# First units of an attention stage in another order, with products that keep TensorE busy between them, before two mixture layers

## The chip, the cores and the metric

One Trainium2 chip, one core of it. The metric is the device time of one execution in microseconds (us); less is better. TensorE (PE) multiplies, with its weight loads (PEld) beside it; VectorE (DVE), ScalarE (ACT) and GpSimd (POOL) work on tiles, and SyncE (SP) issues the DMAs. Each engine takes its instructions in order.

## The reference

A gated linear attention with a running maximum (2 batches, 8 heads, 768 steps, head size 40) feeds two gated layers (1536 tokens, 320 wide, 1536 hidden), all in float32:

```python
for t in range(S):
    m_new = np.maximum(f_gate[:, :, t] + m, i_gate[:, :, t])
    f_stab = np.exp(f_gate[:, :, t] + m - m_new)
    i_stab = np.exp(i_gate[:, :, t] - m_new)
    C = f_stab * C + i_stab * (v k^T)
    n = f_stab * n + i_stab * k
    y[:, :, t] = sigmoid(o_gate) * (C q) / max(|n q|, 1)
x = rms_norm(y) * rms_g
x = (silu(x @ w_gate) * (x @ w_val)) @ w_out
x = (sigmoid(x @ w_gate2) * (x @ w_val2)) @ w_out2
```

The three lines for C, n and y are shortened here; f_stab and i_stab stand for each batch and head.

## The kernel before

**Attention.** The 768 steps are cut into 6 chunks of 128. A unit is one chunk of one batch, all 8 heads; there are 12, and unit u is chunk u // 2 of batch u % 2. Units 0 and 1 need no state from earlier chunks. The running maximum is a scan on DVE: `g_first` scans the first 128 steps (from the small load `fi0`), `g_max` (L178) the other 640. For chunks 1 to 5 the maximum has to lie with one row for each batch, head and chunk (80 rows of 129). Before, `g_move` (L182) writes it to a DRAM tensor `mD` and `g_back` (L186) reads it as 80 rows into `mR`; `g_rest` (L159 to L168) then makes the decay rows of all later chunks. `g_part` splits them into three bf16 parts (two on ACT, L196, one on DVE, L200), and `g_send` (L205) moves the parts to the tiles `rows3` with six DMAs from SP.

A unit goes through: `a_bcast0`/`a_bcast0b` (units 0, 1) or `a_bcast_pe` (later ones; L277, L280), products that lay decay rows over the 128 partitions; `a_exp` (ACT; L313 or L307); `a_scores` (L323, from the tile `qk`); `a_weigh` (DVE, L330); `a_out` (L343, from the tile `nat`, and L339 with the state); `a_wv`, `a_state` (L368), `a_update` (L379) for the state; `a_norm1` to `a_norm3` and `a_flip` (L423 to L425), `a_xt` (ACT, L430; DVE, L431), which put the normed rows transposed and split into `xT`. The causal mask of units below `LATE` is two mask products (L261) ahead of the others; from `LATE` on POOL zeroes the upper triangle after the exponential (L309, two of 128x512).

**Layers.** Tokens are taken in groups of two units; a step is one group with one block of 128 hidden units (12 blocks): `up1` (L460, 16 products of 256 columns), `act1` (ACT L489, DVE L490 and L491, ACT L492, POOL L493) and `dn1` (L471 to L473). The first group (visit 0) goes over the 12 blocks while their weights arrive. A block is two pieces of 544 KB, 24 pieces a layer. A piece is loaded to a raw buffer `wraw` (`w_load`, L98, three buffers); ACT decodes it (`w_pre`: L102 and L109), DVE joins the bits (`w_bits`, L113, last reader of the raw buffer), ACT casts (`w_hi`, L122), DVE subtracts (`w_lo`, L126). Later visits find the weights resident.

**What sets the order.** Everything up to the two `a_xt` of units 0 and 1 is written out by hand in `tc.manual_schedule`, each call adding its instructions at the end of its engines' queues (below: the opening). `keep_warm(n)` there puts n products of 512 columns on PE whose result nobody reads (L673). What follows is placed by a scheduler from due times (`want`). SP's queue is in order too: a DMA that waits holds up all behind it. A DMA takes one of eight semaphores in turn, so it also waits for the DMA eight places earlier.

Of the kernel before, what the change touches and what calls it, by code (L numbers as in the profile page):

```python
# [45 lines left out]

LATE = 4

# [10 lines left out]
def attention_then_two_moe(tc, fi, fir, qk, qt3, nat, w1, w2, rms_g, consts, out):  # L59
# [93 lines left out]
    parts = room[0][0:RR, again + 3 * L:again + 15 * L // 2].bitcast(BF16).rearrange("p (k n) -> p k n", k=3)  # L153
    ph = early[0:BH, 768:768 + L]
    col0, colR = early[:, 896:896 + 2 * BH], small(128, RR, "colR")
# [24 lines left out]

    def g_move():
        nc.sync.dma_start(out=mD, in_=mS[:, L:])  # L182

    def g_back():
        win = bass.AP(tensor=mD.tensor, offset=mD.offset, ap=[[S - L + 1, BH], [L, NR], [1, L + 1]])
        nc.sync.dma_start(out=mR, in_=win)  # L186

    def g_rest():
        g_cum(fiR[:, 0, :], fiR[:, 1, :], mR, phR, uR, RR, False)
        g_aw(fiR[:, 1, :], mR, phR, uR, aR, wsR, RR)  # L190

# [50 lines left out]
    def a_load(u, parts=(0, 1, 2, 3)):  # L242
        d = X.setdefault(u, {})
        if 0 in parts:
            d["qk"] = ap.tile([QR, 2, 4, L], F32, tag="qk", name="qk")
            nc.sync.dma_start(out=d["qk"], in_=qk[u])
        if 1 in parts:
            d["nat"] = ap.tile([128, NAT], F32, tag="nat", name="nat")
            nc.sync.dma_start(out=d["nat"][:, 9 * D:], in_=nat[u, :, 9 * D:])
        if 3 in parts:  # L250
            nc.sync.dma_start(out=d["nat"][:, 0:9 * D], in_=nat[u, :, 0:9 * D])
        if u >= B and 2 in parts:
            d["qt"] = ap.tile([KR, NG, L], F32, tag="qt", name="qt")
            nc.sync.dma_start(out=d["qt"], in_=qt3[u])
# [181 lines left out]
    def a_flip(u):  # L436
        X[u]["T"] = flip(X[u]["y"], X[u]["y"][:, 256:DP])
# [99 lines left out]
    def act2(g, m, gt, vl):  # L537
        if G2[g][1] == 2:
            th = mp.tile([128, 256], F32, tag="th", name="th")
            hT = hts[1, g, m] = mp.tile([128, 2, 256], F32R, tag="hT", name="hT", bufs=3)  # L540
        else:
            th = p2[0].tile([128, 512], F32, tag="th2", name="th2")
            hT = hts[1, g, m] = p2[0].tile([128, 2, 512], F32R, tag="hT2", name="hT2", bufs=3)
# [93 lines left out]
    with tc.manual_schedule(engines=set(engines)):  # L637
        nc.vector.memset(junk, 0.0)
        nc.sync.dma_start(out=fi0, in_=fi[:, :, 0:L])
        nc.scalar.dma_start(out=fiS, in_=fi[:, :, L:])  # L640
        a_load(0, (0,))
        w_load(0, 0, 0)
        nc.scalar.copy(tiny, junk[:, 0:1])
        for t, fill in ((ident, 1.0), (identb, 1.0)):
# [33 lines left out]
        g_max()
        w_pre(0, 0, 0)
        w_load(0, 0, 1)  # L680
        a_load(1, (0,))
        a_load(0, (1,))
        g_move()
        nc.sync.dma_start(out=fiR, in_=fir)
        g_back()
        w_load(0, 1, 0)
        a_load(1, (1,))
        w_load(0, 1, 1)
        nc.sync.dma_start(out=gB, in_=rms_g.partition_broadcast(128))
        nc.sync.dma_start(out=cst, in_=consts)  # L690
        a_load(0, (3,))
# [4 lines left out]
        w_bits(0, 0, 0)
        a_load(1, (3,))
        a_scores(0)
        keep_warm(wm[1])
        a_weigh(0)  # L700
        a_gate(0)
        w_hi(0, 0, 0)
        w_pre(0, 0, 1)
# [8 lines left out]
        a_scores(1)
        g_rest()
        a_out(0)
        a_wv(0)
        w_pre(0, 1, 0)
        g_exp()
        g_part(0)
        g_part(1)
        for k in range(3):  # L720
            g_send(k)
        a_weigh(1)
        w_hi(0, 0, 1)
        w_lo(0, 0, 1)
        a_gate(1)
        g_dec()
        a_norm1(0)
        a_norm1b(0)
        keep_warm(wm[3])
        a_out(1)  # L730
        a_norm1(1)
        a_norm1c(0)
        a_norm1b(1)
        a_norm2(0)
        a_bcast_pe(2)
        a_norm1c(1)
        a_norm2(1)
        keep_warm(wm[4])
        g_cols()
        a_norm3(0)  # L740
        a_flip(0)
# [123 lines left out]
```

## Time and profile before

| | us |
|---|---|
| three runs | 528.14, 524.8, 527.47; median 527.47 |
| profiled execution, its own time | 524.49 |
| span in that profile, first to last instruction | 522.7 |
| outside the span | 1.8 |

The profile is one execution. Its views used here: busy time in chosen stretches, the instructions of an engine in order of time (start, length, count, idle time before it and what ended it), groups of instructions by line, and the chain that ended last. A clock of 1.00 is 2.4 GHz on TensorE, 0.50 is 1.2 GHz. SPq is SP issuing a DMA; the length there is the issuing, not the transfer.

### The profile page before, as it was taken

Reading aid. Unit: us, or ns where it says so; the run is one execution under the profiler, and the core shown is the slowest. Engines: PE = TensorE matmul, PEld = TensorE weight load, DVE = VectorE, ACT = ScalarE, POOL = GpSimd, SP = SyncE. Lnnn points to the kernel's source line nnn. Section 1 sums busy time; section 2 is a strip of 40 time slices with the busy share of each in tenths; the row PEclk is TensorE's granted clock in tenths of the full one; section 3 lists DMA queues with packets and bytes.
Section 4 is the critical chain, followed back from the end, with each engine's and each line's share of the span. In section 5 each row is a group of like instructions: output and inputs, shape, how many; then the busy total and the mean of one; then the engine's idle time right before and its main releaser. Section 6 shows DMA issues by size and latency. Waiting matters only on the chain.

```text
span 522.7 us, 9043 instructions
## 1 busy us (share of the span) xinstructions
PE 503.7 (96%) x3576; PEld 466.8 (89%) x3576; DVE 260.4 (50%) x540; ACT 232.0 (44%) x518; POOL 105.3 (20%) x164
## 2 busy tenths in 40 slices
PE   7889899999999999999999899999999999999996
PEld 5668799999999999999999899998888888888996
DVE  5668789744255445557665646533233233222332
ACT  4667889733233333326576657442222222221322
POOL 7013135443243243232221211110000000000000
PEclk9769979999999999999999999999999999999999
DMA  6588787711041030102153242000000010000100
GB/s 193 182 255 298 246 262 231 240 55 41 1 112 44 25 114 16 41 2 85 35 198 113 92 165 87 1 1 25 1 1 2 0 51 0 1 0 1 51 1 26
DMA packets 15752, 43.09 MB, mean 82 GB/s; under 512 B 1822, under 2 KB 6734, under 8 KB 15710
## 3 DMA queue, kind: packets, MB, share of 16 engines
q1 hardware_dynamic: 15518, 42.27, 25.4%
q8 instruction: 28, 0.46, 0.4%
q10 hardware_dynamic: 192, 0.25, 0.1%
q14 instruction: 14, 0.11, 0.1%
HBM read 40.32 MB, written 2.01 MB: 81 GB/s over the span
## 4 chain that ended last, share of the span: by engine, by line
PE 76%; DMA 10%; ACT 6%; DVE 5%; issue 2%; SPq 0%; ACTq 0%; DVEq 0%
PE up L460 34%; DMA wraw<-in_w_dram 9%; PE sc L460 9%; PE dn L471 5%; PE dn L473 5%; PE dn L472 5%; PE at L343 4%; PE sc L323 2%; DVE wT L113 2%; PE at L471 2%; PE at L472 2%; PE at L473 2%; ACT wT L102 2%; ACT wH L122 2%; ACT wraw L109 1%
## 5 line engine op out<-in xcount | busy, mean ns | idle before, releaser
L460 PE MATMUL up<-xT,wH 128*128 128x256 f32 x940 | 165.4, 290 | 4.2 <-DVE th L491 4.0
L460 PEld LDWEIGHTS up<-xT,wH 128*128 128x128 f32 x940 | 136.0, 192 | 7.5 <-DVE th L491 5.4
L460 PE MATMUL up<-xT,wL 128*128 128x256 f32 x564 | 101.2, 287 | 0.3 <-DVE wL L126 0.3
L493 POOL TENSOR_TENSOR hT<-th,hT 128x256 fp32r<-128x256 f32 x72 | 57.7, 802 | 152.0 <-ACT hT L492 112.7
L460 PEld LDWEIGHTS up<-xT,wL 128*128 128x128 f32 x564 | 82.3, 192 | 0.7 <-DVE wL L126 0.5
L471 PE MATMUL dn<-wH,hT 128*128 128x320 f32 x184 | 58.1, 316 | 0.0
L490 DVE SCALAR_TENSOR_TENSOR th<-th,up 128x256 f32<-128x256 f32 x72 | 30.1, 418 | 56.2 <-ACT th L489 55.8
L472 PE MATMUL dn<-wL,hT 128*128 128x320 f32 x184 | 57.4, 313 | 0.0
L473 PE MATMUL dn<-wH,hT 128*128 128x320 f32 x184 | 56.9, 316 | 0.0
L544 ACT ACTIVATE th<-up 128x256 f32<-128x256 f32 (+1 forms) x48 | 23.4, 488 | 72.8 <-PE up L460 72.8
L545 DVE SCALAR_TENSOR_TENSOR th<-th,sc 128x512 f32<-128x512 f32 x24 | 16.5, 687 | 64.1 <-PE sc L460 63.9
L546 ACT CAST hT<-th 128x256 fp32r<-128x256 f32 (+1 forms) x48 | 24.6, 513 | 49.9 <-DVE th L545 49.8
L489 ACT ACTIVATE th<-up 128x256 f32<-128x256 f32 x72 | 27.3, 380 | 41.3 <-PE up L460 39.9
L109 ACT ACTIVATE wraw<-wraw 128x544 int32<-128x544 uint16 x48 | 34.0, 708 | 25.4 <-DMA wraw<-in_w_dram 25.0
L492 ACT CAST hT<-th 128x256 fp32r<-128x256 f32 x72 | 29.1, 404 | 34.6 <-DVE th L491 34.6
L113 DVE SCALAR_TENSOR_TENSOR wT<-wT,wraw 128x544 int32<-128x544 int32 x48 | 36.9, 772 | 12.8 <-ACT wT L102 7.7
L547 DVE TENSOR_TENSOR hT<-th,hT 128x256 fp32r<-128x256 f32 (+1 forms) x48 | 28.1, 585 | 25.0 <-ACT hT L546 24.9
L126 DVE TENSOR_TENSOR wL<-wT,wH 128x544 fp32r<-128x544 f32 x46 | 34.2, 770 | 7.1 <-ACT wH L122 6.9
L471 PEld LDWEIGHTS dn<-wH,hT 128*128 128x128 f32 x184 | 35.0, 190 | 1.2
L102 ACT ACTIVATE wT<-wraw 128x544 f32<-128x544 f32 x48 | 33.2, 702 | 6.2 <-DMA wraw<-in_w_dram 5.9
L472 PEld LDWEIGHTS dn<-wL,hT 128*128 128x128 f32 x184 | 34.9, 190 | 0.9
L473 PEld LDWEIGHTS dn<-wH,hT 128*128 128x128 f32 x184 | 34.3, 189 | 0.3 <-issue 0.2
(184 smaller groups left out, 821.5 us busy)
## 6 DMA issues: line engine op xcount, KB each, us to landing
wraw<-in_w_dram SPq DMA_DIRECT2D x48, 544.0 KB, 4.8
qk<-in_qk_dram SPq DMA_DIRECT2D x12, 416.0 KB
nat<-in_nat_dram SPq DMA_DIRECT2D x12, 324.0 KB, 2.8
nat<-in_nat_dram SPq DMA_DIRECT2D x12, 180.0 KB, 6.3
qt<-in_qt_dram SPq DMA_DIRECT2D x10, 180.0 KB, 2.8
out_dram<-x2n SPq DMA_DIRECT2D x11, 160.0 KB, 1.9
rows<-x2n SPq DMA_DIRECT2D x6, 30.0 KB
gB<-in_rms_g_dram SPq DMA_DIRECT2D x1, 160.0 KB
```

The costliest lines, as they stand in the source:

```text
L102: nc.scalar.activation(t.bitcast(F32), wraw[moe, m, p][:, :, 1].bitcast(F32), AF.Prelu, scale=2.0 ** -112, alpha=2.0 ** 32)
L109: nc.scalar.activation(raw[:, :, 0], top, AF.Copy, scale=2.0 ** -13, bias=2.0 ** -14 - 0.5)
L113: nc.vector.scalar_tensor_tensor(out=t, in0=t, scalar=3, in1=raw[:, :, 0], op0=ALU.logical_shift_left, op1=ALU.bitwise_or)
L126: nc.vector.tensor_tensor(out=wL[moe, m][:, sl], in0=wT.pop((moe, m, p)).bitcast(F32), in1=wH[moe, m][:, sl].bitcast(F32), op=ALU.subtract)
L460: mm = nc.tensor.matmul(o, lhsT=a, rhs=b, start=(n == 0), stop=(n == 7))
L471: nc.tensor.matmul(o, lhsT=hi, rhs=wo[0], start=first, stop=False)
L472: nc.tensor.matmul(o, lhsT=hi, rhs=wo[1], start=False, stop=False)
L473: pe_last[0] = nc.tensor.matmul(o, lhsT=lo, rhs=wo[0], start=False, stop=last)
L490: nc.vector.scalar_tensor_tensor(out=th, in0=th, scalar=1.0, in1=gt, op0=ALU.add, op1=ALU.mult)
L492: nc.scalar.copy(hT[:, 0, :], th)
L493: nc.gpsimd.tensor_tensor(out=hT[:, 1, :], in0=th, in1=hT[:, 0, :].bitcast(F32), op=ALU.subtract)
L547: nc.vector.tensor_tensor(out=hT[:, 1, :], in0=th, in1=hT[:, 0, :].bitcast(F32), op=ALU.subtract)
```

## The change

The opening is written anew: all loads of units 0 and 1 and the first four weight pieces are issued ahead of the computation; the maximum is scanned later; its 80 rows are made by five products with selection matrices (`selR`) into PSUM instead of the way through DRAM; ACT does the exponentials and the decay rows ahead of most weight pieces; the keep-warm products stand at other places (6, 5, 4, 8, 4 of them; before 6, 2, 0, 5, 4 and none at the last two places). The states of units 0 and 1 are placed earlier (that of unit 0 in the opening, that of unit 1 first thing after it). `LATE` goes from 4 to 2, so units 2 and 3 are masked on POOL and lose two mask products each. Half of the `rows3` transfers go out from POOL. `wraw` has four buffers (and `th2`, of the second layer, one instead of two). `qk` is 104 partitions of which 64 to 103 and 0 to 39 carry data; now the two ranges of 40 are loaded (320 KB) by two DMAs, before all 104 (416 KB) by one.

```diff
-LATE = 4
+LATE = 2
-    uld=9.62, sl=9.1, fl=-6.46, wm=(6, 2, 0, 5, 4, 0, 0), st=1.2,
+    uld=9.62, sl=9.1, fl=-6.46, wm=(6, 5, 4, 8, 4), st=1.2,
...
-        t = wraw[moe, m, p] = mp.tile([128, WP, 2], I32, tag="wraw", name="wraw", bufs=3)
+        t = wraw[moe, m, p] = mp.tile([128, WP, 2], I32, tag="wraw", name="wraw", bufs=4)
...
-    def g_move():
-        nc.sync.dma_start(out=mD, in_=mS[:, L:])
-
-    def g_back():
-        win = bass.AP(tensor=mD.tensor, offset=mD.offset, ap=[[S - L + 1, BH], [L, NR], [1, L + 1]])
-        nc.sync.dma_start(out=mR, in_=win)
+    def g_win():
+        m = psum("dn")[0:RR, 0:L + 1]
+        for c in range(NR):
+            nc.tensor.matmul(m, lhsT=selR[:, c, :], rhs=mS[:, L * (c + 1):L * (c + 2) + 1], start=(c == 0), stop=(c == NR - 1))
+        mR.append(m)
...
-    def g_send(k):
+    def g_send():
         n = H * NR
-        for b in range(B):
-            nc.sync.dma_start(out=rows3[b][k * n:(k + 1) * n].rearrange("p q l -> p (q l)"), in_=parts[b * n:(b + 1) * n, k])
+        for k in range(3):
+            for b, q in ((0, nc.sync), (1, nc.gpsimd)):
+                q.dma_start(out=rows3[b][k * n:(k + 1) * n].rearrange("p q l -> p (q l)"), in_=parts[b * n:(b + 1) * n, k])
...
-            nc.sync.dma_start(out=d["qk"], in_=qk[u])
+            for r in (0, 64):
+                nc.sync.dma_start(out=d["qk"][r:r + D], in_=qk[u, r:r + D])
...
-        a_bcast0(u, "sc")
+        a_bcast0(u, "up" if u == B else "sc")
...
-            th = mp.tile([128, 512], F32, tag="th2", name="th2")
+            th = mp.tile([128, 512], F32, tag="th2", name="th2", bufs=1)
...
-            [a_scale, a_bcast_pe, a_exp] if u > B else [a_scale, a_exp],
+            [a_scale, a_bcast_pe, a_exp],
```

(In the `th2` lines the pool is the second layer's own, `p2[0]`.) The opening, by its calls from the first computation on; loads stand ahead of it:

```python
keep_warm(6); a_bcast0(0); keep_warm(5); g_first(); a_bcast0b(0, 0); g_first_a(); a_bcast0b(0, 1); a_exp(0)
g_max(); a_scores(0); g_win(); a_weigh(0); g_first_ws(); w_pre(0, 0, 0); a_bcast0(1); a_bcast0b(1, 0); a_bcast0b(1, 1)
a_gate(0); g_rest(); a_exp(1); a_wv(0); a_out(0); w_bits(0, 0, 0); g_exp(); a_scores(1); g_part(0); a_norm1(0)
a_weigh(1); a_state(0); w_pre(0, 0, 1); g_part(1); a_norm1b(0); a_norm1c(0); g_send(); a_out(1); a_norm2(0)
w_hi(0, 0, 0); a_gate(1); w_bits(0, 0, 1); a_norm3(0); keep_warm(4); a_flip(0); a_norm1(1); a_norm1b(1); a_norm1c(1)
a_xt(0); w_lo(0, 0, 0); w_hi(0, 0, 1); g_dec(); a_update(0); a_norm2(1); w_pre(0, 1, 0); keep_warm(8); g_cols()
a_norm3(1); keep_warm(4); a_flip(1); w_lo(0, 0, 1); a_xt(1); w_bits(0, 1, 0); w_hi(0, 1, 0); w_lo(0, 1, 0)
```

PE before, from unit 1's mask products to unit 0's `a_out` (L266 feeds unit 1's exponentials, L229 makes a column of weights, L323 are unit 1's scores, L343 is unit 0's `a_out`):

```order
L261 LDWEIGHTS masks
L261 MATMUL up<-masks 128x512
L261 LDWEIGHTS masks
L261 MATMUL up<-masks 128x512
L266 MATMUL up<-x2n,ident 128x128 x8
L229 MATMUL at<-ident,x2n 128x16
L323 MATMUL sc<-qk 128x128 x8
L343 MATMUL at<-nat,E 128x41 x8
```

PE with the change, from unit 0's scores on:

```order
L323 MATMUL sc<-qk 128x128 x8
L183 MATMUL dn<-x2n,early 80x129 x5
L228 MATMUL at<-ident,x2n 128x16
L261 LDWEIGHTS masks
L261 MATMUL up<-masks 128x512
L261 LDWEIGHTS masks
L261 MATMUL up<-masks 128x512
L266 MATMUL up<-x2n,ident 128x128 x8
L343 MATMUL at<-nat,E 128x41 x8
L323 MATMUL sc<-qk 128x128 x8
```

The five products L183 come right behind unit 0's scores, and unit 0's `a_out` (L343) now stands ahead of unit 1's scores.

PE before, around the first step of visit 0 (unit 1's state is L368 with nat, unit 2 is L297, L323 and L339):

```order
L425 MATMUL at<-ident,y 128x128
L368 MATMUL at<-wv,nat 120x123 x2
L368 MATMUL at<-wv,nat 120x82
L460 MATMUL up<-xT,wH_211 128x256 x4
L460 MATMUL up<-xT,wL_212 128x256 x3
L460 MATMUL up<-xT,wH_211 128x256 x5
L460 MATMUL up<-xT,wL_212 128x256 x3
L460 MATMUL up<-xT,wH_211 128x256
L460 MATMUL up<-xT,wH_365 128x256 x4
L460 MATMUL up<-xT,wL_366 128x256 x2
L368 MATMUL at<-wv,nat 120x123 x2
L368 MATMUL at<-wv,nat 120x82
```

PE with the change, the last rows ahead of the first step (all of unit 2 but the state's addition):

```order
L323 MATMUL sc<-qk 128x128 x8
L297 LDWEIGHTS wide
L297 MATMUL at<-rows_0_72,wide 120x128
L297 LDWEIGHTS wide
L297 MATMUL at<-rows_0_72,wide 120x128
L297 LDWEIGHTS wide
L297 MATMUL at<-rows_0_72,wide 120x128
L339 MATMUL at<-St_77,qt 128x123
L368 MATMUL at<-wv,nat 120x123
L339 MATMUL at<-St_77,qt 128x123
L339 MATMUL at<-St_77,qt 128x82
L460 MATMUL up<-xT,wH_314 128x256 x4
```

Unit 2's spreading products, scores and state read, which stood behind the first step or inside the second, now stand ahead of the first.

SP before, from the way through DRAM to the weight piece behind the `rows3` transfers:

```order
L182 DMA mD<-x2n 16x641
L684 DMA x2n<-in_fir_dram 80x256
L186 DMA x2n<-mD 80x1x129
L98 DMA wraw<-in_w_dram 128x1088
L249 DMA nat<-in_nat_dram 128x648
L98 DMA wraw<-in_w_dram 128x1088
```

SP with the change, from the third weight piece to the sixth:

```order
L95 DMA wraw<-in_w_dram 128x1088
L251 DMA nat<-in_nat_dram 128x360
L650 DMA gB<-in_rms_g_dram 128x320
L651 DMA early<-in_consts_dram 80x144
L251 DMA nat<-in_nat_dram 128x360
L95 DMA wraw<-in_w_dram 128x1088
L204 DMA rows_0_72<-x2n 40x384
L204 DMA rows_0_72<-x2n 40x384
L204 DMA rows_0_72<-x2n 40x384
L95 DMA wraw<-in_w_dram 128x1088
```

Four pieces now stand ahead of every transfer that waits for computed data; the first one that waits is the first `rows3` transfer.

## Rows read from the trace of the kernel before

**Rows 1.** The page, busy time of TensorE over the span.

```profile
PE 503.7 (96%) x3576; PEld 466.8 (89%) x3576; DVE 260.4 (50%) x540; ACT 232.0 (44%) x518; POOL 105.3 (20%) x164
```

**Rows 2.** Stretches: length, busy us (instructions) by engine, clock, DMA share, GB/s.

```profile
34.00:46.60 12.60, 12.60 (x100) 11.88 (x99) 9.26 (x18) 10.75 (x21) 2.28 (x3) 0.80 0.87 283
46.60:102.00 55.40, 51.59 (x395) 47.51 (x395) 47.58 (x88) 45.60 (x96) 21.53 (x25) 0.94 0.81 261
102.00:522.70 420.70, 413.03 (x2943) 388.80 (x2941) 182.64 (x385) 158.86 (x359) 69.58 (x104) 1.00 0.13 43
18.70:28.80 10.10, 9.16 (x37) 5.77 (x35) 5.89 (x16) 3.33 (x11) 1.09 (x2) 0.50 0.59 169
32.90:39.00 6.10, 6.10 (x29) 6.10 (x30) 3.89 (x7) 6.02 (x12) 0.74 (x1) 0.50 0.82 262
61.90:64.00 2.10, 0.07 (x1) 0.00 (x0) 1.13 (x4) 2.10 (x6) 0.00 (x0) 1.00 0.98 287
66.80:73.40 6.60, 6.60 (x30) 5.92 (x30) 6.09 (x13) 5.03 (x12) 1.40 (x3) 0.52 0.77 234
```

**Rows 3.** SP in order of time, 9 to 46 us: start, length, line, transfer.

```profile
9.12 0.33 SPq L182 DMA_DIRECT2D mD<-x2n  x1
...
12.72 0.60 SPq L186 DMA_DIRECT2D x2n<-mD  x1
...
19.39 4.79 SPq L205 DMA_DIRECT2D rows<-x2n  x6
...
31.23 0.35 SPq L98 DMA_DIRECT2D wraw<-in_w_dram  x1
...
35.75 0.96 SPq L98 DMA_DIRECT2D wraw<-in_w_dram  x2
...
45.11 10.64 SPq L98 DMA_DIRECT2D wraw<-in_w_dram  x6
```

**Rows 4.** DVE in order of time: the long scan, then the later chunks' decay rows.

```profile
7.33 1.76 DVE L178 TENSOR_TENSOR_SCAN x2n<-x2n 16x640 f32<-16x640 f32 x1
...
16.04 0.82 DVE L159 TENSOR_TENSOR x2n<-x2n 80x128 f32<-80x128 f32 x1
...
18.33 0.29 DVE L168 TENSOR_TENSOR x2n<-x2n 80x128 f32<-80x128 f32 x1
```

**Rows 5.** PE in order of time, opening and first three steps.

```profile
1.06 2.74 PE L673 MATMUL dn<-early 128*128 128x512 bf16 x6 [1.06 <-DVE x2n L172]
...
16.70 2.01 PE L343 MATMUL at<-nat,E 128*128 128x41 f32 x16
...
21.78 3.61 PE L343 MATMUL at<-nat,E 128*128 128x41 f32 x16 [0.94 <-ACT rd L391]
...
31.72 0.33 PE L423 MATMUL at<-ident,y 128*128 128x128 f32 x1 [0.72 <-DVE y L417]
...
34.00 1.20 PE L460 MATMUL up<-xT,wH 128*128 128x256 f32 x4
...
38.84 0.85 PE L368 MATMUL at<-wv,nat 128*120 128x123 f32 x6
...
46.58 0.72 PE L460 MATMUL up<-xT,wH 128*128 128x256 f32 x4
```

**Rows 6.** ACT in order of time: unit 0's exponentials and its gate.

```profile
9.19 2.17 ACT L313 ACTIVATE E<-up,early 128x128 f32<-128x128 f32 x8 [0.57 <-DVE early L224]
12.49 0.47 ACT L348 ACTIVATE nat<-nat 128x320 f32<-128x320 f32 x1 [1.13 <-DMA nat<-in_nat_dram]
```

**Rows 7.** Groups by line, 34 to 102 us: count, busy us, mean ns, idle before.

```profile
L109 ACT ACTIVATE wraw<-wraw 128x544 int32<-128x544 uint16 x25 | 17.8, 711 | 8.0 <-DMA wraw<-in_w_dram 8.0
...
L307 ACT ACTIVATE E<-sc 128x512 f32<-128x512 f32 x10 | 5.6, 599 | 0.0
L309 POOL TENSOR_SCALAR_AFFINE_SELECT E<-E 128x512 f32<-128x512 f32 x6 | 5.5, 933 | 9.6 <-ACT E L307 9.6
```

**Rows 8.** The chain that ended last: start, length of one undisturbed step's 16 products.

```profile
119.13 1.90 PE up L460 x16
```

More of the change, by code (lines that the diff above doesn't have):

```diff
@@ L153, in attention_then_two_moe @@
     parts = room[0][0:RR, again + 3 * L:again + 15 * L // 2].bitcast(BF16).rearrange("p (k n) -> p k n", k=3)
-    ph = early[0:BH, 768:768 + L]
+    selR = early[0:BH, 384:384 + NR * RR].rearrange("p (c r) -> p c r", c=NR)
+    ph = early[0:BH, 928:928 + L]
     col0, colR = early[:, 896:896 + 2 * BH], small(128, RR, "colR")
@@ L541, in act2 @@
         else:
-            th = p2[0].tile([128, 512], F32, tag="th2", name="th2")
+            th = p2[0].tile([128, 512], F32, tag="th2", name="th2", bufs=1)
             hT = hts[1, g, m] = p2[0].tile([128, 2, 512], F32R, tag="hT2", name="hT2", bufs=3)
@@ L641, in attention_then_two_moe @@
         a_load(0, (0,))
+        nc.sync.dma_start(out=fiR, in_=fir)
         w_load(0, 0, 0)
+        a_load(1, (0,))
+        a_load(0, (1,))
+        w_load(0, 0, 1)
+        a_load(1, (1,))
+        w_load(0, 1, 0)
+        a_load(0, (3,))
+        nc.sync.dma_start(out=gB, in_=rms_g.partition_broadcast(128))
+        nc.sync.dma_start(out=cst, in_=consts)
+        a_load(1, (3,))
+        w_load(0, 1, 1)
         nc.scalar.copy(tiny, junk[:, 0:1])
@@ L664, in attention_then_two_moe @@
         nc.gpsimd.tensor_copy(blk, blk9[:, 0:NV])
+        nc.gpsimd.memset(selR, 0.0)
+        nc.gpsimd.affine_select(out=selR, in_=selR, pattern=[[-1, NR], [1, RR]], compare_op=ALU.not_equal,
+                                fill=1.0, base=0, channel_multiplier=-NR)
         for b in range(B):
             nc.gpsimd.memset(St[b], 0.0)
-        for c in range(NR):
-            nc.gpsimd.tensor_copy(wide[:, c].rearrange("p (h d) -> p h d", d=D), picked(c, 9, D))
         warm = psum("dn")
@@ L676, in attention_then_two_moe @@
         a_bcast0(0)
+        keep_warm(wm[1])
         g_first()
[L678 to L691, printed above, removed]
         a_bcast0b(0, 0)
@@ L695, in attention_then_two_moe @@
         a_exp(0)
[L696 to L697 removed]
+        g_max()
         a_scores(0)
[L699 removed]
+        g_win()
         a_weigh(0)
[L701 to L703 removed]
+        g_first_ws()
+        w_pre(0, 0, 0)
         a_bcast0(1)
@@ L706, in attention_then_two_moe @@
         a_bcast0b(1, 1)
+        a_gate(0)
+        g_rest()
+        a_exp(1)
+        a_wv(0)
+        for c in range(NR):
+            nc.gpsimd.tensor_copy(wide[:, c].rearrange("p (h d) -> p h d", d=D), picked(c, 9, D))
+        a_out(0)
+        w_bits(0, 0, 0)
+        g_exp()
+        a_scores(1)
+        g_part(0)
+        a_norm1(0)
+        a_weigh(1)
+        a_state(0)
+        w_pre(0, 0, 1)
+        g_part(1)
+        a_norm1b(0)
+        a_norm1c(0)
+        g_send()
+        a_out(1)
+        a_norm2(0)
+        w_hi(0, 0, 0)
+        a_gate(1)
         w_bits(0, 0, 1)
-        g_first_ws()
-        a_exp(1)
+        a_norm3(0)
         keep_warm(wm[2])
+        a_flip(0)
+        a_norm1(1)
+        a_norm1b(1)
+        a_norm1c(1)
+        a_xt(0)
         w_lo(0, 0, 0)
[L712 to L715, printed above, removed]
+        w_hi(0, 0, 1)
+        g_dec()
+        a_update(0)
+        a_norm2(1)
         w_pre(0, 1, 0)
[L717 to L723, printed above, removed]
-        w_lo(0, 0, 1)
[L725 to L741, printed above, removed]
+        keep_warm(wm[3])
+        g_cols()
+        a_norm3(1)
+        keep_warm(wm[4])
+        a_flip(1)
+        w_lo(0, 0, 1)
+        a_xt(1)
         w_bits(0, 1, 0)
-        keep_warm(wm[5])
-        a_norm3(1)
-        a_xt(0)
         w_hi(0, 1, 0)
-        a_flip(1)
         w_lo(0, 1, 0)
-        a_xt(1)
         marks = [next(i for i in reversed(nc.cur_bb.bb.instructions) if i.engine == e) for e in engines]
@@ L755, in attention_then_two_moe @@
     for u in range(B):
-        want(t_slot(0) + T["st"] + u, lambda: a_state(u), *[lambda: a_wv(1)] * (u == 0), lambda: a_update(u))
+        want(t_slot(0) + T["st"] + u, *[lambda: a_wv(1), lambda: a_state(1), lambda: a_update(1)] * u)
     for c in range(1, NC):
```

9 lines of the change are left out of this document (3 added, 6 removed).

## The prediction

> **What bounds the kernel now.** I read the page's busy times first: TensorE is busy 96% of the span [rows 1], so time comes back only where TensorE stands still or runs at half its clock. The busy time by stretch says where that is. From 102 us on TensorE is busy 413.03 of 420.70 us at full clock, with DVE and ACT under half busy and the transfers at 0.13 [rows 2]: that stage is TensorE's own, and the change takes nothing out of it. Ahead of it lie the opening, whose end is the first step at 34.00 [rows 5], and visit 0, up to 102, in which the 24 pieces of the first layer's weights arrive. There no engine is the bound alone. From 46.6 to 102 TensorE is busy 51.59 of 55.40 us, DVE 47.58, ACT 45.60, the transfers 0.81 [rows 2].
>
> Then I look for lost TensorE time. It runs at 1.2 GHz from 18.7 to 28.8, from 32.9 to 39.0 and from 66.8 to 73.4 [rows 2]; the last fall follows 2.1 us from 61.9 in which it did next to nothing. What half clock costs is seen in the same 16 products of `a_out`: 2.01 us at 16.70, 3.61 us at 21.78 [rows 5].
>
> Last come the engines in order of time, for what holds the opening. DVE starts the decay rows of the later chunks at 16.04 [rows 4], after a way through DRAM issued at 9.12 and read back from 12.72 [rows 3]. ACT waits for a transfer before unit 0's gate until 12.49 [rows 6]. SP is held by the six transfers of the parts from 19.39 for 4.79 us, and issues the next pieces that count at 31.23 and 35.75 [rows 3].
>
> **The change, part by part.** All times are of the profiled execution.
>
> *Start.* Nothing before unit 0's first products depends on the new order but five more keep-warm products: 6 took 2.74 us, some 0.43 each [rows 5], so at most 2.1 us more, of which 1.7 was idle. The 640-column scan of 1.76 us [rows 4] no longer stands between unit 0's column and its exponentials. These start at about 8.0 instead of 9.19, and the eight end at 10.1 [rows 6].
>
> *Maximum by products.* The scan runs from 7.85 to 9.6. Unit 0's scores end at 10.3 as before. Five products of 129 columns follow. No row shows this shape. From below they are free beside idle time; from above they are ten passes at the rate of `a_out` at half clock, 3.61/16 = 0.23 us, 2.3 us in all [rows 5]. I take the rate at full clock, 2.01/16 = 0.126 us: 1.25 us, so the rows lie in PSUM at 11.7. DVE starts them at 11.95, after one short copy, instead of 16.04 [rows 4]: 4.1 us earlier. Ready 2.6 us later (16.04 to 18.62 before), at 14.5.
>
> *To the end of the opening.* Before, it took from 18.62 to 31.72 [rows 4, 5], 13.1 us, from there to the transposes of unit 1. The same steps now follow, with one more weight conversion of 0.71 us [rows 7] ahead of the second part on ACT: 14.5 + 13.1 + 0.7 = 28.3. That is 3.4 us earlier, less than the 4.1 gained. The state of unit 0 (L368) lies inside; that of unit 1, which came at 38.84 [rows 5], now follows at 28.9.
>
> *First step.* Unit 2's spreading products lie in the buffers of the `up` tag, so the first step waits until ACT has taken its first half. ACT has, in order, the cast of unit 1's rows (to 29.4), a cast that waits for DVE's join (to 31.4), five conversions that follow each other every 0.6 us (34.4), then unit 2's exponentials at 0.6 each [rows 7]. So the first step starts at 35.0, a microsecond later than before. This is the new wait, and what is queued behind it is all of TensorE. Its cost is covered: unit 2's spread, scores and state read, and unit 1's state, are done by then, while before they stood behind 34.00.
>
> *To the third step.* From 35.0: 1.9 us for the first step [rows 8], 0.4 for the state's addition, 0.8 for the start of the second step, 1.1 for unit 3's spread, 1.2 for the rest of the second step, 0.9 for unit 2's out: 41.3. The weights of the third step must be there. Behind unit 2's exponentials (35.4) ACT has eight instructions of 0.45 to 0.6 us to their last cast, 39.7, and DVE 0.65 more: 40.35, in time. Before, the third step started at 46.58 [rows 5], because 6.1 us of the way ran at 1.2 GHz [rows 2]. **Term: 46.6 - 41.3 = 5.3 us.** I take the new order at full clock there, since nothing is idle from the flip of unit 1 on but 0.7 us. At half clock it would be some 3 us later, and I keep that for the range.
>
> *Visit 0 behind it.* TensorE's own work from 46.6 to 102 at full clock is 51.59 less half of the 6.6 us at 1.2 GHz, 48.3 us; the stage took 55.4. So at most 7.1 us can come back, and nothing need. For it: ACT waited 8.0 us for pieces [rows 7], and with four raw buffers and earlier issue (seventh piece at about 31, before in the pair at 35.75 [rows 3]) most of these waits end. Against it: ACT and DVE are then the next late ones. Walking two steps further I find ACT full without a pause, and the fourth and fifth steps 4 to 5 us ahead. Units 2 and 3 also lose their four mask products, but pay with four runs on POOL of 0.93 us [rows 7], which DVE waits for in the middle of its weight work (about 2 us, at 34 to 38). **Term: 1.2 us** of the 7.1, a sixth; the ends are -3 (ACT later than walked) and 7.1.
>
> *The other edits.* POOL's three transfers have no row; SP's six took 4.79 us, 0.8 each [rows 3]. Between 0.4 and three times that, POOL is done by 25, and what it does next is unit 1's scale at 27: nothing. One `th2` buffer instead of two: the tanh of a step fires a step after the last, with DVE under half busy [rows 2]: nothing; without that cover 24 steps would each pay part of a microsecond, which I leave to the range.
>
> *qk.* By bytes it is 96 KB a unit, 0.77 MB for the eight units loaded up to 102, at 261 GB/s [rows 2] 2.9 us of transfer. It lies beside TensorE at a share of 0.81, so I put nothing in the sum. The Trainium skill ("DMA: Bandwidth & Descriptors", section on why a DMA increments its semaphore by 16) says that a transfer uses the largest number of engines up to 16 that divides its outer size, the lowest-numbered ones. By that rule 104 rows go over 13 engines at 32 KB each, and twice 40 rows over the same 10, again 32 KB each: nothing would be saved, and the sum would be the same. No row here separates engines.
>
> **The sum.** 5.3 + 1.2 = 6.5 us off the profiled execution's 524.49 (its span of 522.7 and 1.8 around it): 518.0. The median of the three runs is 527.47, 3.0 above that execution, and two of the three are near it. I put half of the difference on the sum: 519.5.
>
> **Rivals.**
>
> *A, given back in visit 0.* The third step is early, but the rate is then ACT's (45.60 us busy of 55.40, with waits of its own order besides), or the clock stays low as it did from 18.7 [rows 2] and the third step gains only 2. For it: three engines above 80% in that stage. Against: ACT's 8.0 us of waits for pieces, which the change attacks. The gain is 1 to 4 us, 524.5.
>
> *B, more.* The two microseconds of standing still at 61.9 and the fall of the clock after them go as well: 2.1 + 3.3 more, 11.9 in all, 514.5. For it: ACT behind a late piece is what ended that idle time by the trace, and pieces come earlier now. Against: scores and exponentials of units 4 and 5 still share two buffers.
>
> *C, slower.* On SP, unit 3's `nat` now stands ahead of the seventh piece and waits for unit 1's state, which is behind unit 1's transposes at the end of a chain over DVE, ACT and POOL. Before, the pieces of the pair at 35.75 stood ahead of that wait. If the chain ended at 40 instead of 28.9, the seventh piece would be issued at 40, 4.3 us late, and the fourth step with it, while the clock falls for want of work, which costs 3.3 as at 66.8: 530 or above. It decides from about 36; the walk leaves 7 us.
>
> *D, the change doesn't do what it says:* keep-warm products are there and TensorE still falls to 1.2 GHz before the first step. That is the second half of A.
>
> **How the numbers follow.** A measurement of this kernel tells about 1% from no change, so faster means below 522.2. My forecast has 0.47 (517 to 522.5; 0.43 of it below the bound), A with D 0.28 (nearly all within 1%), B 0.18, C 0.07. Faster: 0.43 + 0.18 + 0.01 = 0.62. Same: 0.04 + 0.26 + 0.01 = 0.31. Slower: 0.07. The range reaches through A up to 526.5 and below B's middle, to 512.
>
> **What would show it.** Right: decay rows on DVE near 12; unit 1's transposes near 28; the first step near 35 behind an exponential on ACT; the third near 41; clock 1.00 from 30 to 60; ACT's waits for pieces in visit 0 well below 8.0. Wrong: the third step after 44; SP held past 33 at unit 3's `nat`; ACT or DVE over 90% busy from 41 to 90 with TensorE waiting for weights (A); the last 420 us longer than now, which would speak against the single `th2`.

## The result and the profile after

Measured: 521.38 us (median of 20 runs, 518.93 to 531.03) against 527.03 for the kernel before (20 runs, 522.12 to 532.03), a ratio of 0.9904, 95% interval 0.9879 to 0.9928. That is 5.6 us by the medians. The profiled execution took 520.35, 4.1 less than the one before; its span is 518.6. The ratio, here and below, leaves out runs that are more than 1.5% above the fastest of their kernel. The forecast was 519.5, and the sum 6.5.

The page of the changed kernel, the row that answers to [rows 1]:

```profile
PE 505.1 (97%) x3592; PEld 467.3 (90%) x3592; DVE 261.0 (50%) x540; ACT 231.3 (45%) x518; POOL 108.7 (21%) x173
```

Its stretches, columns as in [rows 2]: length, busy us (instructions) of PE, PEld, DVE, ACT, POOL, then TensorE's clock, DMA share, GB/s.

```profile
34.00:46.60 12.60, 11.37 (x84) 10.89 (x85) 8.46 (x15) 10.44 (x21) 2.08 (x4) 0.86 0.79 240
46.60:102.00 55.40, 52.79 (x417) 48.44 (x416) 49.22 (x95) 48.48 (x105) 24.23 (x32) 1.00 0.75 250
102.00:518.60 416.60, 411.09 (x2906) 386.74 (x2904) 180.59 (x379) 155.81 (x351) 67.42 (x100) 1.00 0.13 41
19.50:27.00 7.50, 7.47 (x29) 5.01 (x30) 4.68 (x12) 4.04 (x11) 0.98 (x1) 0.54 0.85 265
37.00:40.50 3.50, 3.50 (x20) 3.50 (x18) 3.14 (x5) 2.79 (x6) 0.81 (x2) 0.51 1.01 273
187.00:191.00 4.00, 4.00 (x23) 3.54 (x23) 2.51 (x9) 1.13 (x4) 0.54 (x1) 0.57 0.38 103
```

From 46.6 to 102 the clock is 1.00 where it was 0.94, and DVE and ACT are fuller. At 1.2 GHz TensorE now runs from about 20 to 27, from 37 to 40.5, and, new, from 187 to 191, in a stretch in which the row calls it busy throughout.

DVE, PE and ACT in order of time, the opening and the first steps (start, length, engine, line, idle time before it and what ended it); they answer to [rows 4] and [rows 5]:

```profile
7.80 1.53 DVE L176 TENSOR_TENSOR_SCAN x2n<-x2n 16x640 f32<-16x640 f32 x1
...
11.83 0.27 DVE L157 TENSOR_TENSOR x2n<-x2n,dn 80x128 f32<-80x128 f32 x1
...
32.87 0.73 DVE L123 TENSOR_TENSOR wL<-wT,wH 128x544 fp32r<-128x544 f32 x1 [0.71 <-ACT wH L119]
33.62 0.49 DVE L379 TENSOR_TENSOR St<-blk,at 120x328 f32<-120x328 f32 x1
34.04 0.55 DVE L300 TENSOR_TENSOR qt<-qt,at 120x384 f32<-120x384 f32 x1
```

```profile
10.33 1.33 PE L183 MATMUL dn<-x2n,early 16*80 16x129 f32 x10
...
29.53 0.33 PE L423 MATMUL at<-ident,y 128*128 128x128 f32 x1 [0.71 <-DVE y L417]
...
34.64 0.48 PE L339 MATMUL at<-St,qt 120*128 120x123 f32 x2 [1.66 <-DVE qt L300]
...
36.34 0.74 PE L460 MATMUL up<-xT,wH 128*128 128x256 f32 x4 [0.59 <-ACT E L307]
36.92 0.72 PE L460 MATMUL up<-xT,wL 128*128 128x256 f32 x3
37.44 1.27 PE L460 MATMUL up<-xT,wH 128*128 128x256 f32 x5
...
45.13 0.72 PE L460 MATMUL up<-xT,wH 128*128 128x256 f32 x4
```

```profile
32.19 0.64 ACT L119 CAST wH<-wT 128x544 fp32r<-128x544 f32 x1 [1.58 <-DVE wT L110]
...
35.68 1.09 ACT L307 ACTIVATE E<-up 128x512 f32<-128x512 f32 x2
```

The decay rows start at 11.83 (forecast 11.95), unit 1's transposes come at 29.53 (28.3), the first step at 36.34 (35.0) behind ACT's exponentials, as foreseen. The third step stands at 45.13, where 41.3 was forecast and 46.58 was before.

SP in order of time, and the group of ACT's conversions of pieces from 34 to 102, beside [rows 3] and [rows 7]:

```profile
16.11 3.22 SPq L204 DMA_DIRECT2D rows<-x2n  x3
...
30.84 0.35 SPq L249 DMA_DIRECT2D nat<-in_nat_dram  x1
...
32.22 0.33 SPq L95 DMA_DIRECT2D wraw<-in_w_dram  x1
```

```profile
L106 ACT ACTIVATE wraw<-wraw 128x544 int32<-128x544 uint16 x28 | 19.8, 712 | 6.9 <-DMA wraw<-in_w_dram 6.9
```

SP was held at unit 3's `nat`, as foreseen, but only until 30.84, right behind unit 1's state (5.6 us by its waits); the seventh piece goes out at 32.22 (forecast about 31). ACT still waits 6.9 us for pieces (8.0 before).

**Where the time came from.** To find it I set each step's start of the tanh on ACT (L489, in the second layer L544) beside the same step before; steps are counted from 0 through both layers. It is one execution of each kernel. A difference that changes between two steps is time won or lost between them.

| step | before, us | after, us | difference | between this row and the one above |
|---|---|---|---|---|
| 0 | 38.9 | 42.5 | +3.6 | the later first step |
| 2 | 51.4 | 51.7 | +0.3 | unit 2's work already done |
| 8 | 83.9 | 79.7 | -4.2 | no stop of TensorE at 61.9, no fall of the clock at 66 |
| 24 | 143.0 | 138.6 | -4.4 | |
| 36 | 197.3 | 195.7 | -1.6 | of the 2.8, 1.5 at the fall of the clock at 187 |
| 75 | 325.9 | 322.8 | -3.1 | second layer's weights arrive |
| 115 | 504.8 | 501.4 | -3.4 | |

The runs say the same in another way. A run's span times its granted clock is an estimate of what it would take at 2.4 GHz throughout, as if all of it went by TensorE's clock; the rest of the span is counted as lost to the clock. Of the kernel before, the medians in four groups of runs are 511.1 to 512.8 us at full clock and 10.5 to 12.1 lost; of the changed one 511.9 and 7.8. By that count most of the gain is clock, and hardly any of it less work or less waiting. (The mean granted clock of the changed kernel's 20 runs goes from 0.968 to 0.993, and their time varies by about 2%; where the others fell is not on record.)

### The profile page after: what moved, and what is told of

It is laid out like the page before. It is cut to its first block, busy times and chain, and to the rows that moved or that the text cites. A ratio compares the mean times of both kernels' runs of the same rounds, so it can differ in the third digit from the quotient of the medians.

```text
span 518.6 us, 9096 instructions
## 1 busy us (share of the span) xinstructions
PE 505.1 (97%) x3592; PEld 467.3 (90%) x3592; DVE 261.0 (50%) x540; ACT 231.3 (45%) x518; POOL 108.7 (21%) x173
## 4 chain that ended last, share of the span: by engine, by line
PE 75%; DMA 10%; ACT 8%; DVE 4%; issue 2%; POOL 0%; SPq 0%; ACTq 0%; POOLq 0%
PE up L460 32%; PE sc L460 9%; DMA wraw<-in_w_dram 9%; PE dn L471 5%; PE dn L472 5%; PE dn L473 5%; PE at L343 4%; PE sc L323 3%; ACT wT L99 2%; ACT wH L119 2%; ACT wraw L106 2%; PE dn L685 2%; DVE wT L110 2%; PE at L472 2%; PE at L471 2%
## 5 line engine op out<-in xcount | busy, mean ns | idle before, releaser
L460 PE MATMUL up<-xT,wH 128*128 128x256 f32 x940 | 163.7, 288 | 3.8 <-DVE th L491 1.8
L544 ACT ACTIVATE th<-up 128x256 f32<-128x256 f32 (+1 forms) x48 | 23.6, 491 | 72.4 <-PE up L460 72.4
L489 ACT ACTIVATE th<-up 128x256 f32<-128x256 f32 x72 | 27.4, 381 | 41.8 <-PE up L460 41.8
L547 DVE TENSOR_TENSOR hT<-th,hT 128x256 fp32r<-128x256 f32 (+1 forms) x48 | 28.3, 589 | 25.0 <-ACT hT L546 24.9
L123 DVE TENSOR_TENSOR wL<-wT,wH 128x544 fp32r<-128x544 f32 x46 | 33.2, 755 | 9.8 <-ACT wH L119 9.6
```

The costliest lines, as they stand in the source:

```text
L123: nc.vector.tensor_tensor(out=wL[moe, m][:, sl], in0=wT.pop((moe, m, p)).bitcast(F32), in1=wH[moe, m][:, sl].bitcast(F32), op=ALU.subtract)
L460: mm = nc.tensor.matmul(o, lhsT=a, rhs=b, start=(n == 0), stop=(n == 7))
L547: nc.vector.tensor_tensor(out=hT[:, 1, :], in0=th, in1=hT[:, 0, :].bitcast(F32), op=ALU.subtract)
```

## The experiments

First theory: each part acts where the prediction put it, so that undoing one gives back its own share. Against it: the gain belongs to one part, and undoing another costs nothing. What each means in numbers stands in the expectations. The table sums up all runs, each timed in five rounds against the kernel before. "Step 24" and "step 115" are the differences to before in the profile, as above; the two columns behind them are the medians of the runs' time at full clock and of what they lost to it.

| run | us | ratio, 95% interval | step 24 | step 115 | at full clock | lost |
|---|---|---|---|---|---|---|
| the change | 521.38 | 0.9904 (0.9879-0.9928) | -4.4 | -3.4 | 511.9 | 7.8 |
| raw3 | 527.74 | 1.0037 (1.0004-1.007) | -3.4 | +3.2 | 514.0 | 12.1 |
| b_raw4 | 525.04 | 1.0015 (0.9977-1.0052) | -3.8 | +0.4 | 512.5 | 9.9 |
| dram | 531.75 | 1.0112 (1.0055-1.0168) | +4.8 | +7.7 | 516.3 | 13.0 |
| qk104 | 524.78 | 0.9986 (0.9954-1.0019) | -1.7 | -0.1 | 513.5 | 9.9 |
| nowarm | 529.48 | 1.009 (1.0052-1.0127) | -0.2 | +5.4 | 510.8 | 16.6 |
| late4 | 525.83 | 1.0008 (0.9976-1.004) | -3.0 | +1.3 | 513.5 | 10.5 |
| b_late2 | 530.3 | 1.0114 (1.006-1.0168) | +0.5 | +5.1 | 513.4 | 17.4 |
| early2 | 523.28 | 0.9955 (0.9917-0.9994) | -6.3 | -0.2 | 510.7 | 10.4 |
| early2_7 | 518.63 | 0.988 (0.983-0.9929) | -5.8 | -5.5 | 508.8 | 8.3 |
| late4_7 | 521.54 | 0.993 (0.9901-0.9959) | -0.6 | -0.9 | 511.2 | 8.3 |
| raw3_7 | 520.98 | 0.9935 (0.99-0.997) | -3.8 | -3.5 | 511.0 | 8.3 |
| early2_79 | 518.25 | 0.9894 (0.9849-0.9938) | -5.9 | -7.8 | 508.2 | 8.8 |

### One part undone, or done alone

**raw3**: the change with three raw buffers (`bufs=4` to `bufs=3` in `wraw`).

> The changed kernel with three raw buffers instead of four, nothing else. Theory O (the new opening brings the gain, the fourth buffer little): still about 4.5 us under the kernel before, ratio 0.991 to 0.993. Theory R (the fourth raw buffer brings it, because pieces come earlier in visit 0 and again in the second layer's loading at 255 to 320 us): most of the gain is gone, ratio 0.998 or above, ACT's waits for pieces from 34 to 102 us back at 8 us or more, TensorE idle again around 60 and from 280 to 310.

Up to step 24 it is 1.0 us behind the change, in the end 6.6. ACT's waits for pieces did not come back with the third buffer; they are shorter than with four (5.0 us, 6.9 in the change). **b_raw4** is the mirror: the kernel before with `wraw` of four buffers and `th2` of one.

> The kernel before with four raw buffers and one th2 buffer, its opening, LATE, qk load and maximum as before. Theory O: within 1.5 us of the kernel before, ratio 0.997 or above. Theory R: 3 to 5 us faster, ratio 0.990 to 0.994. The single th2 buffer costs nothing by both; if it did, this would come out slower.

ACT's conversions of pieces from 34 to 102, raw3 first, then b_raw4:

```profile
L106 ACT ACTIVATE wraw<-wraw 128x544 int32<-128x544 uint16 x26 | 18.3, 703 | 5.0 <-DMA wraw<-in_w_dram 5.0
```

```profile
L109 ACT ACTIVATE wraw<-wraw 128x544 int32<-128x544 uint16 x27 | 19.2, 714 | 8.2 <-DMA wraw<-in_w_dram 8.0
```

Alone the buffers are worth nothing that can be measured in the total. The single `th2` costs nothing in the profile either: from step 75 to step 115, the steps of the second layer, b_raw4 goes from 0.5 to 0.4 us behind before. But at step 24 b_raw4, with the old opening, stands 3.8 us ahead: the stop at 61.9 and the fall at 66 are gone in it, as they are in raw3. So either the new opening or the fourth buffer is enough to lose them in a profile, and b_raw4 gives the time back at falls from 187.5 and from 252.5.

**dram**: the rows of the maximum through DRAM again, in the new opening.

```diff
...
-        for c in range(NR):
-            nc.tensor.matmul(m, lhsT=selR[:, c, :], rhs=mS[:, L * (c + 1):L * (c + 2) + 1], ...)
...
+        nc.sync.dma_start(out=mD, in_=mS[:, L:])
...
+        nc.sync.dma_start(out=mR[0], in_=win)
```

> The changed kernel with the maximum's 80 rows taken through DRAM again instead of the five products; the loads stay ahead of that on SP. By the sum of the prediction the decay rows then start on DVE about 4 us later (near 16 instead of 11.8), and unit 1's transposes, the first step and the third step 3 to 4 us later: ratio 0.996 to 0.998. If the opening's end doesn't carry through visit 0 (theory R), at most 1.5 us of that reaches the end: ratio 0.990 to 0.994.

DVE's decay rows in this run, and PE behind them:

```profile
19.95 0.29 DVE L160 TENSOR_TENSOR x2n<-x2n 80x128 f32<-80x128 f32 x1 [8.45 <-DMA x2n<-mD]
```

```profile
25.93 3.61 PE L345 MATMUL at<-nat,E 128*128 128x41 f32 x16 [8.72 <-issue]
...
43.13 0.75 PE L462 MATMUL up<-xT,wH 128*128 128x256 f32 x4 [0.58 <-ACT E L309]
```

With four pieces issued ahead, the way through DRAM costs 8.1 us at the decay rows (19.95 against 11.83), twice the forecast, and 6.8 at the first step. The write to DRAM goes out at 12.49, behind the fourth piece; before, it went at 9.12. Of the parts undone this is the dearest up to step 24 (-4.4 to +4.8): with the loads issued first, the opening needs the products. (One of the six runs took 2751.97 us; no trace of it is kept, and without it the median is 531.28.)

**nowarm**: `wm=(6, 0, 0, 0, 0)` in place of `(6, 5, 4, 8, 4)`.

> The changed kernel with the first six keep-warm products alone, the other 21 left out. If they hold the clock where it counts: TensorE at 1.2 GHz through the first steps, the third step 2 to 3 us later than 45.1, ratio 0.994 to 0.997. If they don't (the changed kernel fell to 1.2 GHz at about 19.5 and 37 although they were there): within 1 us of the changed kernel, ratio 0.989 to 0.992, or better, since unit 0's transposes no longer stand behind four products at 1.2 GHz.

One stretch of it:

```profile
18.50:36.00 17.50, 11.86 (x58) 9.98 (x58) 12.43 (x30) 6.45 (x16) 4.15 (x7) 0.51 0.61 183
```

Half clock from 18.5 to 36. By the runs it loses 16.6 us to the clock instead of 7.8, and takes 510.8 at full clock, no more than the change: what it loses is clock. Not all of that is the keep-warm products' own work, though. In the profile it is 4.2 us behind the change at step 24, and about as much again by step 26, at a fall from 148.5 to 159 that it shares with other runs (below). How much they are worth with that fall kept out no run here shows.

**qk104**: one load of 104 rows of `qk` instead of two of 40.

> The changed kernel with qk loaded as all 104 rows by one transfer again. If bytes count: 1.15 MB more over the kernel, visit 0 later by up to 2 us, ratio 0.992 to 0.995. If a transfer's time goes by the engines it is spread over (13 for 104 rows, 10 for 40, both 32 KB on the busiest): no difference, ratio 0.989 to 0.992, and in the opening the first four pieces land at the same time as with the two loads of 40 rows.

TensorE's order is the same as with the change up to 95 us and differs widely only behind 150. Unit 1's transposes are 0.4 us later (29.94), the clock falls at 17.5 instead of 20 and once more from 75.5 to 79.5. The edit put down as nothing is worth 3.4 us by the medians, 2.1 of them lost to the clock, and the intervals of the ratios lie apart; whether by the transfers or by the order behind them is not shown.

**late4** and **b_late2**: `LATE` back to 4 in the change, and 2 in the kernel before.

> The changed kernel with LATE back at 4: units 2 and 3 masked by four products on TensorE and not on POOL. If POOL's two runs ahead of unit 2's weighing are on the path (DVE waited 1.3 us for them), the third step comes about 1 us earlier and the whole is up to 1 us faster, ratio 0.987 to 0.990; if TensorE's 0.9 us for the products counts instead, 0.9 us slower, ratio 0.991 to 0.994.

> The kernel before with LATE at 2 alone. By TensorE's time 0.8 to 0.9 us faster, ratio 0.998 to 0.999; by DVE's wait for POOL in the middle of the weight work 1 us slower, ratio 1.001 to 1.003.

Set alone, masking units 2 and 3 on POOL makes the kernel before slower by 1.1%; taken out of the change, it costs the whole gain as well. The same edit cannot be bad and good by its own work.

**early2**: unit 2's spreading products and exponentials in the opening, in place of the last four keep-warm products, against the waits at 34.64 and 36.34.

> The changed kernel with unit 2's spreading products and exponentials moved into the opening, ahead of unit 1's transposes, in the place of the last four keep-warm products. In the changed kernel the first step waits for these exponentials behind five weight conversions on ACT (36.34 instead of 34 in the kernel before). If that wait is what cost the forecast 4 us at the third step: the first step at 34 to 35, the third step 1 to 2 us before 45.1, ratio 0.986 to 0.989. If the third step waits for its weights anyway: no difference, ratio 0.989 to 0.992.

The first steps are earlier, and step 24 stands 6.3 us ahead of before. At step 115 only 0.2 of it is left.

So neither reading holds. Five single undoings (raw3, dram, nowarm, qk104, late4) each lose nearly all of the gain or more, and in raw3, late4 and early2 most goes behind step 24, where `LATE` and the opening have nothing left to do and the buffers have only from 240 us on, when the second layer's weights load.

### What they share: two kinds of products in turn

The stretch in which they lose is much the same, 140 to 164 us in all. late4, PE in order of time, units 6 and 7 (a product stands as two passes in these rows, so the eight scores of a unit are x16):

```profile
144.71 0.48 PE L323 MATMUL sc<-qk 40*128 40x128 f32 x2
145.13 0.41 PE L343 MATMUL at<-nat,E 128*128 128x41 f32 x2
145.47 0.49 PE L323 MATMUL sc<-qk 40*128 40x128 f32 x4
145.90 0.42 PE L343 MATMUL at<-nat,E 128*128 128x41 f32 x2
146.24 0.69 PE L323 MATMUL sc<-qk 40*128 40x128 f32 x2
146.86 0.65 PE L343 MATMUL at<-nat,E 128*128 128x41 f32 x2
```

The scores of unit 7 (40 rows) and the out products of unit 6 (128 rows; ahead of these its state reads, L339) take turns. The scheduler places what it reckons to be ready, and any edit ahead can change that: in the built order the two change over 13 times in late4, 14 in raw3, early2, dram and nowarm, 10 in b_late2, but twice in before, the change, qk104 and b_raw4. All six that take turns have a fall of the clock there, between 143 (early2) and 164 (dram); of the four that don't, qk104 alone has one, at 150.5 to 154.5, so this is not the only cause of a fall. The change's own rows for the same products:

```profile
143.64 0.80 PE L339 MATMUL at<-St,qt 120*128 120x123 f32 x6
144.27 1.47 PE L343 MATMUL at<-nat,E 128*128 128x41 f32 x12
145.67 1.71 PE L323 MATMUL sc<-qk 40*128 40x128 f32 x16
147.31 0.64 PE L343 MATMUL at<-nat,E 128*128 128x41 f32 x4
```

Theory S: the taking of turns is what loses the time, by itself and by the clock that falls in it (8.3 us in late4, 142.87 to 151.19, of which the last 5 at 1.2 GHz, against 4.1 here). To test it, one edge is added to three of the kernels that lost, and nothing else:

```diff
-        for h, hh in order:
+        with tc.issue_after(X[6]["last"].ins) if u == 7 else ExitStack():
+            for h, hh in order:
...
```

(`last` is the last out product of a unit: unit 7's scores now stand behind all of unit 6's.)

> The changed kernel with LATE back at 4 (units 2 and 3 masked on PE), and unit 7's scores products behind the last of unit 6's out products. In run late4 the two alternate (13 switches) from 142.9 to 151.2 us, with 1.2 GHz from 146 to 157. Theory S: LATE itself costs what it cost up to the 24th step, 1.5 us, and the rest of late4's loss was the alternation: the block takes about 4.3 us instead of 8.3, no 1.2 GHz between 146 and 157, the 26th step 1 to 2.5 us later than in the changed kernel instead of 5.8, and the time is 522 (520.5 to 523.5), ratio 0.993. Theory R (masks on PE or late units cost all of it): time as in late4, 525.8, ratio 1.001, with 1.2 GHz at the same place.

> The changed kernel with three raw buffers, and unit 7's scores products behind the last of unit 6's out products. In run raw3 the two alternate (14 switches) with 1.2 GHz from 146 to 153.5 us. Theory S: three buffers cost 1.0 us up to the 24th step and 3 to 4 us while the second layer's weights load (250 to 300 us), and the 2 to 3 us between were the alternation: no 1.2 GHz between 140 and 160, the 34th step 0.5 to 1.5 us later than in the changed kernel instead of 3.4, the time 525 (523.5 to 526.5), ratio 0.998. Theory R (three buffers alone cost all 6.6 us): the time as in raw3, 527.7, ratio 1.004.

> The kernel of run early2 (unit 2's spreading products and exponentials in the opening) with one edge more: unit 7's eight scores products stand behind the last of unit 6's out products. In early2 the two alternate one by one (14 switches) from 139.8 to 147.3 us, with 1.2 GHz from 143 to 150.5; by the built order nothing ahead of 139 changes. Theory S (the alternation is what loses the time): that block takes about 4.5 us instead of 7.5, the stretch at 1.2 GHz from 143 to 150.5 goes, the step ahead of it (the 24th) is where it was in early2 (6.3 us ahead of before), the 36th is 2 to 3 us earlier than in early2, and the time is 520.5 (519 to 522), ratio 0.990. Theory R (the order of the two does not matter, the loss comes from a late input or the clock falls there anyway): 36th step and time as in early2 within 1 us, 523.3, ratio 0.9955.

Groups by line, columns as in [rows 7]: late4 from 142.8 to 151.2, then late4_7 from 145 to 149 (all of the same 16 passes each).

```profile
L323 PE MATMUL sc<-qk 40*128 40x128 f32 x16 | 4.2, 382 | 0.0
L343 PE MATMUL at<-nat,E 128*128 128x41 f32 x16 | 4.1, 388 | 0.0
```

```profile
L344 PE MATMUL at<-nat,E 128*128 128x41 f32 x16 | 1.9, 280 | 0.0
...
L324 PE MATMUL sc<-qk 40*128 40x128 f32 x16 | 1.2, 285 | 0.0
```

The same 11 us of both, late4 first:

```profile
146.00:157.00 11.00, 11.00 (x48) 9.83 (x49) 3.59 (x8) 1.85 (x6) 0.89 (x2) 0.53 0.29 90
```

```profile
146.00:157.00 11.00, 11.00 (x98) 10.54 (x98) 7.05 (x18) 4.19 (x12) 3.64 (x6) 1.00 0.31 95
```

Busy throughout in both, but at 0.53 of the clock with 48 products in one, at 1.00 with 98 in the other. That is the lesson of the page's busy share: it cannot tell the two apart. late4_7 is 4.3 us faster than late4, early2_7 4.7 than early2, raw3_7 6.8 than raw3 by the medians, some 4.1, 3.9 and 5.4 by the ratios to the kernel before in the same rounds, and none has a fall between 140 and 160. (The intervals of early2 and early2_7 just touch, the others lie apart.) Theory R, that the part undone costs it all, has fallen for late4 and raw3, and with the profile for early2. The edge leaves TensorE's order ahead of unit 7's scores as it was, but behind them the scheduler places some later products otherwise as well, so that the gain need not all be the turns. late4_7 came out as forecast (522). early2_7 came out better (520.5 forecast), and so did raw3_7 (525 forecast): with unit 7's scores in one piece, three raw buffers are not told from four by the total. In the profile they may still cost something: 3.5 us ahead of the change at step 45, raw3_7 is level with it at step 65, after this stop behind ACT's waits for pieces, and a fall of the clock from 250 to 254. (From 240 to 300 us these waits come to 10.5 us in either kernel.)

```profile
246.17 0.70 ACT L106 ACTIVATE wraw<-wraw 128x544 int32<-128x544 uint16 x1 [0.99 <-DMA wraw<-in_w_dram]
...
248.44 0.38 PE L472 MATMUL sc<-wH,hT 128*128 128x320 f32 x1 [2.61 <-DVE x2T L433]
```

So neither three buffers nor masks on TensorE are told from the change by the total (0.9935 and 0.993 beside 0.9904, with intervals that overlap). dram, nowarm and b_late2 take turns too and were not run with the edge: what they lose behind step 24 is not shown to be their own edit's.

How far one profile can be trusted is seen here as well. late4 and late4_7 have the same order on TensorE up to 142 us, and still stand 2.4 us apart at step 24, because the clock fell at other places; raw3 and raw3_7, early2 and early2_7 are 0.4 and 0.5 apart. A difference of one or two microseconds at step 24 in the table tells nothing.

**early2_79**: the same edge for unit 9 (`u in (7, 9)` with `X[u - 1]`), against the fall of the clock at 183.5 that early2_7 has left.

> The kernel of run early2_7 with the same edge for unit 9: its scores products stand behind the last of unit 8's out products. In early2_7 the two stand in blocks there (8 out, 4 scores pairs, 8 out, scores) from 179.3 to 183.8 us, and TensorE runs at 1.2 GHz from 183.5 to 187.5. By the built order nothing ahead of 179 changes. Theory S, carried on to blocks: the fall at 183.5 goes with the blocks, 1.7 us, and the time is 517 (515.5 to 518.5), ratio 0.985. Rival N (two changes between blocks are too few to matter; late4_7 and raw3_7 hold the same products in blocks of 12 and 16 at 184 and 180 us without a fall): the 36th step within 0.7 us of early2_7's, a fall at about the same place or somewhere near, time 518.6, ratio 0.988.

Its rows, and the fall was again at 183.5 to 187.5:

```profile
179.22 1.93 PE L344 MATMUL at<-nat,E 128*128 128x41 f32 x16
181.09 1.16 PE L324 MATMUL sc<-qk 40*128 40x128 f32 x8
182.60 1.16 PE L324 MATMUL sc<-qk 40*128 40x128 f32 x8
```

Rival N holds: a few changes between long blocks are not what makes that fall, and 518.25 is not told from 518.63. What does make it stays open: in the change the block of unit 8 and 9 at 182.7 (12 out passes, 16 scores, 4 out) is followed by a fall at 187, in raw3_7 the same block at 180.1 by none.

early2_7 and early2_79 beat the kernel before (0.988 and 0.9894). Beside the change's 0.9904 the intervals overlap: their medians are 3 us lower, which these runs don't establish.

## Why the prediction was right, and where its steps were wrong

**The opening held.** Scan, rows by products, decay rows and transposes came within 1.3 us of the walk, and dram shows that the products carry it. SP's wait at unit 3's `nat` ended at 30.84, far from the 36 at which rival C would decide.

**The third step: the term of 5.3 us measured 1.45** (46.58 to 45.13). The new wait was named and is there, but mis-sized: ACT's exponentials start at 35.68, not 34.4. The five conversions ahead of them took 2.94 us as reckoned, but the cast ahead of those waited 1.58 us for DVE's join and ended at 32.8 instead of 31.4; the join came behind unit 1's transposed rows, which were 1.2 us late. A second wait was missed. "Unit 2's spread, scores and state read ... are done by then" was wrong for the state read: it needs `qt`, which DVE scales at 34.04, behind a weight subtraction (L123) that itself waits for ACT's cast. TensorE stood still for 1.66 and 0.59 us, and then the step "I take the new order at full clock there" failed: 1.2 GHz from 37 to 40.5. The way adds up: first step 1.3 late, 1.7 for the clock, 0.8 because unit 2's out products, reckoned at 0.9, came mixed with state products over 1.73 us (43.40 to 45.13): 41.3 + 3.8 = 45.1. On ACT even the 1.45 is not there: the tanh of that step starts at 51.7, 0.3 later than before.

**Visit 0: the term of 1.2 us measured 3.0** (-4.4 at step 24, less the 1.45). The reason given for it, that four buffers end ACT's waits for pieces, is not borne out: they went from 8.0 to 6.9 only, are 5.0 with three buffers (raw3) and 8.2 with four in the old kernel (b_raw4). What came back is what rival B named, the stop at 61.9 and the fall of the clock at 66.8 with its 3.3 us. (By its own terms B's time is 519.5 - 5.4 = 514.1, not 514.5.) That they are gone in b_raw4 too, which is no faster in the end, leaves open which part of the change does it and how much of the total it is.

**"The change takes nothing out of" the last 420 us: wrong in both directions.** 2.8 us were given back by step 36, 1.5 of them at the fall at 187, and 1.5 came again by step 75, while the second layer's weights arrive. The two nearly cancel, which helped the total.

**Edits put at nothing.** Right for the single `th2`: b_raw4 has it and is not slower. Wrong for `qk` by the total (3.4 us by the medians). The Trainium skill ("DMA: Bandwidth & Descriptors", why a DMA increments its semaphore by 16) would have given nothing there as well, by an estimate from its rule on how many engines a transfer uses; the measured difference speaks against leaving it at that, but no row separates engines, much of it is clock, and the order on TensorE is not the same. `wraw` and `LATE` I placed by the waits they end or make; their real weight was that they changed the scheduler's order.

So the sum of 6.5 us came near the 5.6 measured with terms that were off by 4 and 2 us in opposite directions; that the total came so near is in part luck. What it got right is the kind of gain: from the first step to 102 us less time at 1.2 GHz, at the price of a new wait ahead of the first step.

## What to carry to other kernels

Where a scheduler sets the order, an edit's local worth and its effect on the total are different things: compare the starts of the same step in both traces, and blame the edit only for what goes where it acts. Read the granted clock beside the busy share; a stretch at 100% can take twice as long as it needs. If one unlucky order is found, hold it with a single edge before judging any other edit, since otherwise each experiment measures the order again.

## What the runs showed of the hardware that was not expected

- Products of 40 rows and of 128 rows in turn cost about 0.19 us a pass at full clock (0.76 us for four, 144.71 to 145.47 in late4); in blocks they cost 0.07 to 0.11 (1.16/16 in late4_7, 1.71/16 in the change) and 0.12 (1.92/16). The Trainium skill ("TensorE: Matmul & The Clock Gate", the steps of a matmul) says that weight loads are pulled ahead of running products where their row groups don't conflict or where they go to the background weight buffer. Scores that stay among themselves, 40 rows from row 0 and 40 from row 64 in turn, would fit the first, but no run here shows that it is the cause.
- TensorE fell to 1.2 GHz with no idle time in its rows: at 146 in late4 after 3 us of products in turn, and at 187 in the change after none.
- Runs of one kernel lie up to 12 us apart. Over the change's 20 runs the time at full clock spreads over 6.1 us (508.6 to 514.7) and what the clock takes over 13.3 (3.6 to 16.9): most of the spread is the clock too.
